# A chunked mLSTM feeding a two-layer MLP on one core: the program's head is reordered

## The chip, the cores and the metric

One core of one Trainium2 chip. The metric is the device time of one launch in microseconds (us). The kernel before took 427.0 us as the median of 3 runs (426.79 to 427.44).

## The reference

An mLSTM recurrence over 768 positions for 4 x 8 heads of width 40, and an MLP on its output:

```python
for t in range(S):
    m_new = max(f[t] + m, i[t])
    C = exp(f[t] + m - m_new) * C + exp(i[t] - m_new) * outer(v[t], k[t])
    n = exp(f[t] + m - m_new) * n + exp(i[t] - m_new) * k[t]
    y[t] = sigmoid(o[t]) * (C @ q[t]) / max(abs(n @ q[t]), 1)
x = y as 3072 rows of 320
h = x @ w_in                      # 320 x 2048
out = (h * sigmoid(h)) @ w_out    # 2048 x 320
```

Everything is float32 at the border of the kernel.

## The kernel before, in words

The recurrence is cut into 12 chunks of 64 positions, each in two halves of the batch: 24 **units** (class `Unit`, `u0`, `u1`, ...). A unit makes a matrix of exponents `e` (products with `sel`, `terms`, L433 to L446), exponentiates it to `D` (`expo_act`, L456), multiplies it with the scores `p` = q.k (`scores` L586, `weigh` L613), multiplies the result with v (`values` L641, output `po`), normalises (`norm`, `level`, L707 to L720), multiplies with the output gate (`scale`, L739, output `x`), and carries the state on (`state`, `hold`, `carry`). `xpose` (L856) transposes `x` into `px`; `xputs` (L865 to L872) copies `px` into the MLP's input. In the first MLP step the first 256 of the 320 features go as one float32 copy to `x0` (L865), the other 64 as a high part and a remainder to `xb` (L870, L872).

The MLP works in 8 **steps** (class `Step`) of three units, 384 rows each. In a step, `mm1(fc)` makes one of 16 **groups** of 128 hidden features: for step 0 two products over 256 rows of `w_in` (`wi`, the main part) and two over the remaining 64 rows (`wh`, the **tail**), all added up in one PSUM bank `ph` (L923). `act` takes tanh (L937, ScalarE) and the product with `ph` (`g`, L944, VectorE), and `mm2` multiplies `g` with `w_out` into `pout` (L1017), two groups behind `mm1`. `ph` has two banks, so group 2 needs the bank that `g` of group 0 gives back.

The weights arrive as 64-bit numbers in parts: `i0` to `i7` (w_in), `c0`, `c2`, `c4`, `c6` (tails, one for four groups), `o0` to `o7` (w_out), in the order of the string at L378. `load` issues a part's DMA on SyncE's queue (L283), `rise` widens its two halves on ScalarE (L291, L292), `make` puts them together on VectorE (L315), `halve` splits a tail part into a high part (phase 0, L336) and a remainder (phase 1, L338). `wload(n)` loads the next n parts, `wmake(n)` makes the next n and loads one more after each.

All engines run in the order in which the code is written (both `manual_schedule` lines at the top), each engine's queue in order. So the head, from `u0.load_qk()` to the table `FILL`, is a hand-written order: a call is placed where its instruction should stand in its engine's queue. `FILL[fc]` lists what is put behind group fc of step 0; `FILL[0]` makes the first w_out part, holds unit 2's state and exponentiates unit 3's reach; `FILL[1]` makes part `i2` and exponentiates unit 3 (`expo_act`); `FILL[2]` begins with the scores of unit 3, which take the one PSUM buffer of `couple` in which unit 3's exponents stood.

`gates` yields after each of its pieces, so that `run(1, two)` places one piece of the second pair of chunks (L175 to L193). `small(32)` and `warm(6, ph)` are products of constants with the identity, whose results nobody reads.

Of the kernel before, what the change touches and what calls it, by code (L numbers as in the profile page):

```python
# [8 lines left out]
F32 = mybir.dt.float32  # L9
# [36 lines left out]
def mlstm_mlp_kernel(  # L46
# [217 lines left out]
    class Part:  # L264
# [17 lines left out]
                to, src = self.raw, self.src  # L282
            nc.sync.dma_start(to, src)  # L283

        def rise(self):

            if not wide:
                return
            low, high = self.raw[:, :, :, 0], self.raw[:, :, :, 1]
            h32 = high.bitcast(F32)  # L290
            nc.scalar.activation(h32, h32, AF.Prelu, scale=2.0**-112, alpha=-(2.0**32))  # L291
            nc.scalar.activation(  # L292
                low, self.raw.bitcast(U8)[:, :, :, 3], AF.Copy, scale=1 / 32, bias=-31 / 64
            )
            self.risen = True

        def make(self):
            K, nb, n, nm = self.K, self.nb, self.n, self.nm
# [76 lines left out]
        )  # L375


    order = "c0 i0 i1 o0 i2 c2 o1 i3 o2 c4 i4 o3 i5 o4 c6 i6 o5 i7 o6 o7"  # L378
    parts = [part(x[0], int(x[1])) for x in order.split()]
    nload, nmade = [0], [0]  # L380

# [37 lines left out]
    class Unit:  # L419
# [438 lines left out]
        def xput(self, st):  # L858
            run(2, self.xputs(st))

        def xputs(self, st):
            n, px = self.n, self.px
            cs = slice(n % UPS * UT, (n % UPS + 1) * UT)
            if st.j == 0:
                nc.scalar.copy(st.x0[:, 0:2, cs], px[:, 0:2, :])  # L865
                a = slice(2, 3)
            else:
                a = slice(0, 3)
            hi, lo = st.xh[:, :, cs], st.xl[:, :, cs]
            nc.scalar.copy(hi, px[:, a, :])  # L870
            yield
            self.low = nc.vector.tensor_tensor(  # L872
                out=lo, in0=px[:, a, :], in1=hi.bitcast(F32), op=ALU.subtract
            )

    def run(n, it):
        for _ in range(n):
            next(it, None)

    def pieces(two, n):  # L880
        return (slice(0, n // 2), slice(n // 2, n)) if two else (slice(0, n),)

    class Step:


        def __init__(self, j):
            self.j = j

            if j == 0:
                self.x0 = pb.tile([128, 3, NT], F32, tag="big", name=f"x{j}")  # L890
                both = pb.tile([128, 2, NT], F32R, tag="big", name=f"xb{j}")
                self.xh, self.xl = both[:, 0:1, :], both[:, 1:2, :]
            else:
                self.xh = pb.tile([128, 3, NT], F32R, tag="big", name=f"xh{j}")
                self.xl = pb.tile([128, 3, NT], F32R, tag="big", name=f"xl{j}")
            self.g = {}
            self.po = None

        def mm1(self, fc):
            j = self.j  # L900
            fs = slice(fc * 128, (fc + 1) * 128)
            ph = psH.tile([128, NT], F32, tag="h", name=f"ph{j}_{fc}")
            if j == 0 and fc == 0:
                warm(6, ph)
            if j == 0:
                w = wi[fc // 2]
                b = fc % 2 * 128
                ops = [(w[:, a, b : b + 128], self.x0[:, a, :]) for a in range(2)]
            else:
                w = wl[fc // 2]  # L910
                b = fc % 2 * 128
                ops = []
                for a in range(2):
                    ops += [
                        (wh[:, a, fs], self.xh[:, a, :]),
                        (wh[:, a, fs], self.xl[:, a, :]),
                        (w[:, a, b : b + 128], self.xh[:, a, :]),
                    ]
            z = 2 * (j > 0)
            ops += [(wh[:, 2, fs], self.xh[:, z, :]), (wh[:, 2, fs], self.xl[:, z, :])]  # L920
            for i, (w, x) in enumerate(ops):
                for c in pieces(j == 0 and fc in (0, 1, 2, 3, 12, 13, 14) and i == 1, NT):
                    nc.tensor.matmul(  # L923
                        ph[:, c],
                        w,
                        x[:, c],
                        start=(i == 0),
                        stop=(i == len(ops) - 1),
                        skip_group_check=True,
                    )  # L930

            self.ph = ph
# [178 lines left out]
    u1.load_v()  # L1111
    u2.load_v()
    u1.load_ko()
    wload(2)
    u2.load_ko()
    wload(2)
    for _ in range(2):
        nc.tensor.matmul(
            dummy, ident, ident.unsqueeze(1).broadcast_to([128, 4, 128]), start=True, stop=True
# [7 lines left out]
    u1.mask()  # L1127
    u2.mask(psU.tile([128, H, L], F32, tag="u", name="e2"))
    u0.scores()
    small(32)  # L1130
    u0.expo()
    u0.expo_act()
    u0.keep()
# [26 lines left out]
    u1.place()  # L1160
    u1.values()
    u1.gate()
    u2.gate()
    u1.keys(nc.gpsimd)
    run(1, two)
    u1.norm()
    u1.level()
    u2.place()
    u2.values()
    u1.scale()  # L1170
    u2.keys(nc.gpsimd)
    u0.room()
    u0.xpose()
    u1.state()
    u3.mask(couple("e3")[:, :4, :].rearrange("p b (c t) -> p (b c) t", t=L))
    u3.expo()
    u2.norm()
    u2.level()
    wmake(1)
    u2.scale()  # L1180
    halve(0, nc.gpsimd)
    steps[0] = st = Step(0)
    u0.xput(st)
    u3.load_qk()
    wmake(1)
    u1.xpose()
    u3.reach()
    u1.xput(st)
    u2.room(psU, "u")
    u2.xpose()  # L1190
    u2.xput(st)
    u3.load_kvo()
    wmake(1)
    FILL = {
# [65 lines left out]
    for k in range(FIRST):  # L1260
        j, fc = divmod(k, NFC)
        st, at = steps[j], places(k)
        if j == 0 and fc in KEYS:
            units[KEYS[fc]].keys()
        st.mm1(fc)
        if 0 in at:
            def blocks():
                block(at[0].n)
# [286 lines left out]
```

## Time and profile before

| | |
|---|---|
| median of 3 runs | 427.0 us (426.79 to 427.44) |
| profiled execution | 426.86 us, of which the profile's span is 425.1 us |
| PE busy | 417.6 us, 98% (6864 matmuls, 6864 weight loads) |
| DVE, ACT, POOL busy | 65%, 52%, 31% |
| chain that ended last | PE 77%, "issue" 18%, DVE 2%, ACT 1%, DMA 1% |
| PEclk | 9 (90% or more) in all 40 slices |
| DMA | 57.60 MB; share 8 or 9 tenths in the first five slices |
| queue q8, instructions | 54 packets, 0.88 MB |

PE is TensorE's matrix unit, DVE VectorE, ACT ScalarE, POOL GpSimd, SP SyncE. A share of 98% says that there is little to win by hiding work, and that what PE does not do in time is paid at the end. Slice 1 of 40 is the one with less: PE shows 7 tenths there and 9 in nearly all others. That slice is the head.

### The profile page before, as it was taken

Reading aid. Unit: us, or ns where it says so; the run is one execution under the profiler, and the core shown is the slowest. Engines: PE = TensorE matmul, PEld = TensorE weight load, DVE = VectorE, ACT = ScalarE, POOL = GpSimd, SP = SyncE. Lnnn points to the kernel's source line nnn. Section 1 sums busy time; section 2 is a strip of 40 time slices with the busy share of each in tenths; the row PEclk is TensorE's granted clock in tenths of the full one; section 3 lists DMA queues with packets and bytes.
Section 4 is the critical chain, followed back from the end, with each engine's and each line's share of the span. In section 5 each row is a group of like instructions: output and inputs, shape, how many; then the busy total and the mean of one; then the engine's idle time right before and its main releaser. Section 6 shows DMA issues by size and latency. Waiting matters only on the chain.

```text
span 425.1 us, 16217 instructions
## 1 busy us (share of the span) xinstructions
PE 417.6 (98%) x6864; PEld 389.7 (92%) x6864; DVE 274.5 (65%) x575; ACT 223.0 (52%) x493; POOL 131.6 (31%) x140
## 2 busy tenths in 40 slices
PE   7999999999999999999999999999999999999995
PEld 4777779999999999999999999999999999999995
DVE  5879877987875667477655677466673676444442
ACT  7787777774654454445453544454454434443331
POOL 6754235424432444034431343134530210000000
PEclk9999999999999999999999999999999999999999
DMA  8999989365533755066630774246650321001001
GB/s 267 375 358 242 282 239 287 83 174 142 130 121 98 180 150 155 26 181 179 145 99 26 191 184 133 74 137 144 163 162 2 77 56 39 20 17 32 2 2 48
DMA packets 63401, 57.60 MB, mean 136 GB/s; under 512 B 31808, under 2 KB 49936, under 8 KB 63328
## 3 DMA queue, kind: packets, MB, share of 16 engines
q1 hardware_dynamic: 63056, 56.20, 47.8%
q8 instruction: 54, 0.88, 0.9%
q10 hardware_dynamic: 208, 0.26, 0.2%
q14 instruction: 19, 0.16, 0.1%
q0 software_dynamic: 64, 0.10, 0.1%
HBM read 49.09 MB, written 7.36 MB: 133 GB/s over the span
## 4 chain that ended last, share of the span: by engine, by line
PE 77%; issue 18%; DVE 2%; ACT 1%; DMA 1%; POOL 0%; POOLq 0%; DVEq 0%; ACTq 0%
PE spot L1322 28%; PE pout L1346 26%; PE ph L923 6%; PE pout L1017 6%; PE p L586 3%; PE p L679 2%; PE p L657 2%; PE spot L765 2%; DMA home<-in_ig_dram 1%; DVE D L613 0%; PE p L856 0%; PE px L856 0%; PE po L641 0%; POOL qt L570 0%; DVE home L188 0%
## 5 line engine op out<-in xcount | busy, mean ns | idle before, releaser
L1322 PE MATMUL spot<-xh,wh 64*128 64x384 f32 x660 | 148.7, 339 | 0.0
L1346 PE MATMUL pout<-woh,gh 64*128 64x320 f32 x648 | 128.0, 311 | 0.0
L1346 PE MATMUL pout<-woh,gl 64*128 64x320 f32 x648 | 126.5, 305 | 0.0
L1346 PE MATMUL pout<-wol,gh 64*128 64x320 f32 x648 | 126.1, 304 | 0.0
L961 ACT ACTIVATE th<-spot 128x384 f32<-128x384 f32 x110 | 54.1, 492 | 132.7 <-PE spot L1322 132.5
L1322 PE MATMUL spot<-xl,wh 64*128 64x384 f32 x550 | 122.8, 336 | 0.0
L981 DVE TENSOR_TENSOR gl<-th,gh 128x384 fp32r<-128x384 f32 x113 | 75.3, 666 | 54.9 <-ACT gh L977 44.3
L968 DVE SCALAR_TENSOR_TENSOR th<-th,spot 128x384 f32<-128x384 f32 x110 | 60.6, 551 | 64.1 <-ACT th L961 64.0
L1322 PEld LDWEIGHTS spot<-xh,wh 64*128 64x128 f32 x660 | 98.8, 184 | 2.2 <-ACTq L1302 0.3
L1322 PE MATMUL spot<-xh,wl 64*128 64x384 f32 x440 | 97.7, 333 | 0.0
L1346 PEld LDWEIGHTS pout<-woh,gh 64*128 64x128 f32 x648 | 88.8, 184 | 1.3
L1346 PEld LDWEIGHTS pout<-woh,gl 64*128 64x128 f32 x648 | 88.8, 184 | 0.0
L1346 PEld LDWEIGHTS pout<-wol,gh 64*128 64x128 f32 x648 | 88.6, 184 | 0.0
L977 ACT CAST gh<-th 128x384 fp32r<-128x384 f32 x113 | 58.0, 513 | 39.0 <-DVE th L968 32.8
L1322 PEld LDWEIGHTS spot<-xl,wh 64*128 64x128 f32 x550 | 76.5, 184 | 0.0
L1322 PEld LDWEIGHTS spot<-xh,wl 64*128 64x128 f32 x440 | 64.6, 184 | 0.0
L570 POOL TENSOR_TENSOR qt<-qk,lq 104x512 f32<-104x512 f32 x22 | 29.1, 1321 | 63.1 <-ACT lq L566 62.5
L810 POOL TENSOR_TENSOR Cm<-Cm,lq 104x328 f32<-104x328 f32 x19 | 18.4, 966 | 91.0 <-PE p L679 90.0
L545 POOL TENSOR_TENSOR am<-mask,aT 128x512 f32<-128x512 f32 x20 | 20.9, 1044 | 43.2 <-DVE kw L605 19.4
L553 POOL TENSOR_TENSOR D<-D,am 128x512 f32<-128x512 f32 x20 | 27.7, 1384 | 8.9 <-DMA D<-LFd 5.9
L1017 PE MATMUL pout<-wo,g 128*128 128x320 f32 (+1 forms) x120 | 27.0, 368 | 0.0
L923 PE MATMUL ph<-x,wi 128*128 128x384 f32 (+1 forms) x78 | 23.6, 432 | 0.0
(170 smaller groups left out, 544.9 us busy)
## 6 DMA issues: line engine op xcount, KB each, us to landing
qk<-in_qk_dram SPq DMA_DIRECT2D x24, 512.0 KB, 5.2
ko<-in_ko_dram SPq DMA_DIRECT2D x24, 320.0 KB, 5.1
wro<-in_w_out_dram SPq DMA_DIRECT2D x8, 640.0 KB, 6.3
wri<-in_w_in_dram SPq DMA_DIRECT2D x8, 512.0 KB, 7.4
D<-LFl SPq DMA_DIRECT2D x32, 128.0 KB, 3.5
lq<-LFl SPq DMA_DIRECT2D x32, 128.0 KB, 4.5
vb<-in_vp_dram SPq DMA_DIRECT2D x48, 82.0 KB, 4.7
out_dram<-ob SPq DMA_DIRECT2D x45, 80.0 KB, 2.2
```

Of the source, the lines that this page charges most:

```text
L545: return nc.gpsimd.tensor_tensor(out=self.am, in0=mask.unsqueeze(1).broadcast_to([128, H, L]), in1=aT[:, self.c, self.p, :].unsqueeze(2).b ...
L553: nc.gpsimd.tensor_tensor(out=self.Dm, in0=self.Dm, in1=self.am, op=ALU.add)
L570: nc.gpsimd.tensor_tensor(out=self.qt, in0=self.q[:KS], in1=self.lq[:KS], op=ALU.mult)
L810: nc.gpsimd.tensor_tensor(out=v, in0=heads(Cb[r, a]) if n == NP else v, in1=self.lq[r, :, L - 1].unsqueeze(2).broadcast_to([r.stop - r.sta ...
L923: nc.tensor.matmul(ph[:, c], w, x[:, c], start=(i == 0), stop=(i == len(ops) - 1), skip_group_check=True,)
L961: self.tanh = nc.scalar.activation(th, ph, AF.Tanh, scale=0.5)
L968: nc.vector.scalar_tensor_tensor(out=th, in0=th, scalar=1.0, in1=ph, op0=ALU.add, op1=ALU.mult)
L977: nc.scalar.copy(gh, th)
L981: nc.vector.tensor_tensor(out=gl, in0=th, in1=gh.bitcast(F32), op=ALU.subtract)
L1017: nc.tensor.matmul(self.po[t][:, c], g[:, ts], w[:, c], start=(fc == 0 and i == 0), stop=(last and i == len(ops) - 1), skip_group_check=(j ...
L1322: m = nc.tensor.matmul(spot[g][:, :NT], w, x, start=(h == 0 and i == 0), stop=(h == 1 and i == n - 1), skip_group_check=True,)
L1346: m = nc.tensor.matmul(st.po[t], g[half(h), t * UT : (t + 1) * UT], w[half(h)], start=(f == 0 and i == 0 and (p, h) in ((0, 0), (0, 1), (1 ...
```

## The change

The first two parts in the order of loads change places. The widening of `i0` is taken out of `wmake` and put ahead of unit 2's gate; that of `c0` is cut in two. Unit 2 is normalised before unit 1 is scaled. All three units are transposed before the first copy to the MLP's input, and the copies of the 256 features (`lift`) come ahead of the remainders. The tail's remainder goes from POOL to DVE. One piece of `gates` goes behind all that. `mm1` can make a group's main part and its tail apart: groups 0 and 1 are now main 0, main 1, tail 0, (state of unit 2), tail 1. `small(32)` and `warm(6, ph)` go.

```diff
-        def rise(self):
+        def rise(self, phases=(0, 1)):
...
-    order = "c0 i0 i1 o0 i2 c2 o1 i3 o2 c4 i4 o3 i5 o4 c6 i6 o5 i7 o6 o7"
+    order = "i0 c0 i1 o0 i2 c2 o1 i3 o2 c4 i4 o3 i5 o4 c6 i6 o5 i7 o6 o7"
...
+        def lift(self, st):
+            cs = slice(self.n % UPS * UT, (self.n % UPS + 1) * UT)
+            nc.scalar.copy(st.x0[:, 0:2, cs], self.px[:, 0:2, :])
+            self.lifted = True
...
-            if j == 0 and fc == 0:
-                warm(6, ph)
...
+            main = len(ops) - 2
             for i, (w, x) in enumerate(ops):
+                if (i >= main) not in ends:
+                    continue
...
     u1.load_ko()
-    wload(2)
+    wload(1)
     u2.load_ko()
-    wload(2)
+    wload(3)
...
     u0.scores()
-    small(32)
     u0.expo()
...
     u1.gate()
+    u1.keys(nc.gpsimd)
+    parts[0].rise()
     u2.gate()
-    u1.keys(nc.gpsimd)
-    run(1, two)
     u1.norm()
     u1.level()
     u2.place()
     u2.values()
-    u1.scale()
     u2.keys(nc.gpsimd)
+    u2.norm()
+    u2.level()
     u0.room()
     u0.xpose()
+    u1.scale()
     u1.state()
     u3.mask(couple("e3")[:, :4, :].rearrange("p b (c t) -> p (b c) t", t=L))
     u3.expo()
-    u2.norm()
-    u2.level()
-    wmake(1)
+    u1.xpose()
     u2.scale()
-    halve(0, nc.gpsimd)
-    steps[0] = st = Step(0)
-    u0.xput(st)
-    u3.load_qk()
-    wmake(1)
-    u1.xpose()
-    u3.reach()
-    u1.xput(st)
     u2.room(psU, "u")
     u2.xpose()
-    u2.xput(st)
+    u3.reach()
+    steps[0] = st = Step(0)
+    x0, x1, x2 = (u.xputs(st) for u in (u0, u1, u2))
+    run(1, x0)
+    parts[1].rise((0,))
+    run(1, x1)
+    wmake(1)
+    u3.load_qk()
+    run(1, x0)
+    u2.lift(st)
+    parts[1].rise((1,))
+    run(1, x2)
+    run(1, x1)
+    wmake(1)
+    run(1, x2)
+    halve(0, nc.gpsimd, (0,))
+    halve(0, nc.vector, (1,))
+    run(1, two)
     u3.load_kvo()
     wmake(1)
...
-        st.mm1(fc)
+        if k == 0:
+            st.mm1(0, (0,))
+            st.mm1(1, (0,))
+            st.mm1(0, (1,))
+        else:
+            st.mm1(fc, (1,) if k == 1 else (0, 1))
```

PE at the first two groups, before. In `ph0_1` the first figure is the step and the second the group; `x0` with `wi` is the main part, `xb` with `wh` the tail, `pu2` the state of unit 2 (its remaining rows repeat these two), and the first row stands for six with their weight loads:

```order
L1100 MATMUL ph0_0_526<-maskb_105,identb_104 128x384
L923 MATMUL ph0_0_526<-x0_472,wi0_481 128x384
L923 MATMUL ph0_0_526<-x0_472,wi0_481 128x192 x2
L923 MATMUL ph0_0_526<-xb0_473,wh_106 128x384 x2
L765 MATMUL pu2_u_542<-vb2_145,kw2_426 40x41 x2
L765 MATMUL pu2_o_543<-vb2_145,kw2_426 40x41 x2
L923 MATMUL ph0_1_581<-x0_472,wi0_481 128x384
L923 MATMUL ph0_1_581<-x0_472,wi0_481 128x192 x2
L923 MATMUL ph0_1_581<-xb0_473,wh_106 128x384 x2
L923 MATMUL ph0_2_607<-x0_472,wi1_522 128x384
```

And now:

```order
L935 MATMUL ph0_0_494<-x0_456,wi0_463 128x384
L935 MATMUL ph0_0_494<-x0_456,wi0_463 128x192 x2
L935 MATMUL ph0_1_498<-x0_456,wi0_463 128x384
L935 MATMUL ph0_1_498<-x0_456,wi0_463 128x192 x2
L935 MATMUL ph0_0_494<-xb0_457,wh_106 128x384 x2
L767 MATMUL pu2_u_508<-vb2_145,kw2_391 40x41 x2
L767 MATMUL pu2_o_509<-vb2_145,kw2_391 40x41 x2
L935 MATMUL ph0_1_498<-xb0_457,wh_106 128x384 x2
L935 MATMUL ph0_2_569<-x0_456,wi1_490 128x384
```

The six constant products are gone, and the main part of group 1 stands between the main part and the tail of group 0.

ACT from the gate of unit 1 (`ko1`) to the copies of unit 2, before (`wrc0` is the tail part, `wri0` the w_in part, `px` the transposed units):

```order
L559 ACTIVATE ko1_172<-ko1_172 128x320
L559 ACTIVATE ko2_178<-ko2_178 128x320
L291 ACTIVATE wrc0_174<-wrc0_174 128x256
L292 ACTIVATE wrc0_174<-wrc0_174 128x256
L865 COPY x0_472<-px0_428 128x2x128
L870 CAST xb0_473<-px0_428 128x128
L291 ACTIVATE wri0_176<-wri0_176 128x512
L292 ACTIVATE wri0_176<-wri0_176 128x512
L865 COPY x0_472<-px1_485 128x2x128
L870 CAST xb0_473<-px1_485 128x128
L865 COPY x0_472<-px2_509 128x2x128
L870 CAST xb0_473<-px2_509 128x128
```

And now:

```order
L561 ACTIVATE ko1_172<-ko1_172 128x320
L292 ACTIVATE wri0_174<-wri0_174 128x512
L294 ACTIVATE wri0_174<-wri0_174 128x512
L561 ACTIVATE ko2_176<-ko2_176 128x320
L866 COPY x0_456<-px0_398 128x2x128
L879 CAST xb0_457<-px0_398 128x128
L292 ACTIVATE wrc0_178<-wrc0_178 128x256
L866 COPY x0_456<-px1_427 128x2x128
L879 CAST xb0_457<-px1_427 128x128
L866 COPY x0_456<-px2_435 128x2x128
L294 ACTIVATE wrc0_178<-wrc0_178 128x256
L879 CAST xb0_457<-px2_435 128x128
```

The w_in part is widened ahead of unit 2's gate, and the tail part in two pieces between the copies.

DVE from the weighing of unit 2 (`D2`) on, before (of `norm`, `level` and `scale` only the first instruction is shown here; L188 is the piece of `gates`):

```order
L613 TENSOR_TENSOR D2_305<-p2_357,D2_305 128x512
L188 SCALAR_TENSOR_TENSOR home_110<-home_110 32x128
L707 TENSOR_SCALAR po1_386<-po1_386 128x8
L739 SCALAR_TENSOR_TENSOR x1_422<-ko1_172,po1_386 128x256
L707 TENSOR_SCALAR po2_405<-po2_405 128x8
L315 SCALAR_TENSOR_TENSOR wtc0_460<-wrc0_174 128x256
L739 SCALAR_TENSOR_TENSOR x2_464<-ko2_178,po2_405 128x256
L872 TENSOR_TENSOR xb0_473<-px0_428,xb0_473 128x128
L315 SCALAR_TENSOR_TENSOR wi0_481<-wri0_176 128x512
L872 TENSOR_TENSOR xb0_473<-px1_485,xb0_473 128x128
L872 TENSOR_TENSOR xb0_473<-px2_509,xb0_473 128x128
L315 SCALAR_TENSOR_TENSOR wi1_522<-wri1_180 128x512
```

And now:

```order
L615 TENSOR_TENSOR D2_273<-p2_325,D2_273 128x512
L709 TENSOR_SCALAR po1_354<-po1_354 128x8
L709 TENSOR_SCALAR po2_374<-po2_374 128x8
L741 SCALAR_TENSOR_TENSOR x1_402<-ko1_172,po1_354 128x256
L741 SCALAR_TENSOR_TENSOR x2_431<-ko2_176,po2_374 128x256
L317 SCALAR_TENSOR_TENSOR wi0_463<-wri0_174 128x512
L881 TENSOR_TENSOR xb0_457<-px0_398,xb0_457 128x128
L881 TENSOR_TENSOR xb0_457<-px1_427,xb0_457 128x128
L317 SCALAR_TENSOR_TENSOR wtc0_474<-wrc0_178 128x256
L340 TENSOR_TENSOR wh_106<-wtc0_474,wh_106 64x2x128 x2
L188 SCALAR_TENSOR_TENSOR home_110<-home_110 32x128
L317 SCALAR_TENSOR_TENSOR wi1_490<-wri1_180 128x512
```

Unit 2 is normalised right after unit 1, `wi0` comes ahead of all remainders, the tail's split (L340) is new here, and the gate piece went from the second place to the last but one.

## Rows read from the trace of the kernel before

**Rows 1.** Busy time by stretches: us, busy (x instructions) of each engine, PEclk, DMA.
```profile
5.00:10.00 5.00, 4.18 (x104) 2.93 (x102) 3.69 (x12) 3.31 (x7) 2.57 (x9) 1.00 1.05 339
...
30.00:35.00 5.00, 5.00 (x20) 3.53 (x19) 4.05 (x7) 4.89 (x13) 1.04 (x1) 1.00 0.98 229
```

**Rows 2.** PE in order of time, 24 to 28 us: start, us, what [idle before].
```profile
24.25 1.46 PE L923 MATMUL ph<-x,wi 128*128 128x384 f32 x6
...
25.89 1.78 PE L1017 MATMUL pout<-wo,g 128*128 128x320 f32 x6
27.77 0.69 PE L586 MATMUL p<-qk 40*64 40x64 f32 x32
```

**Rows 3.** ACT in order of time, 16 to 28 us.
```profile
16.23 0.47 ACT L559 ACTIVATE ko<-ko 128x320 f32<-128x320 f32 x1 [1.24 <-DMA ko<-in_ko_dram]
...
18.40 0.67 ACT L292 ACTIVATE wri<-wri 128x512 uint32<-128x512 uint8 x1
...
19.47 0.37 ACT L865 COPY x<-px 128x256 f32<-128x256 f32 x1
...
22.16 0.49 ACT L937 ACTIVATE th<-ph 128x384 f32<-128x384 f32 x1 [1.03 <-PE ph L923]
...
27.11 0.60 ACT L456 ACTIVATE D<-e 128x512 f32<-128x512 f32 x1
```

**Rows 4.** PE in order of time, 0 to 22 us.
```profile
1.36 3.71 PE L1118 MATMUL dummy<-ident 128*128 128x512 f32 x4 [1.36 <-POOL ident masks.py:199]
...
6.29 1.11 PE L1104 MATMUL dummy<-maskb,identb 128*128 128x64 bf16 x32
8.21 0.39 PE L442 MATMUL e<-terms,home 96*128 96x64 bf16 x8 [0.82 <-DVE terms L170]
...
13.39 0.73 PE L641 MATMUL po<-vb,D 128*64 128x82 f32 x16
14.68 0.79 PE L641 MATMUL po<-vb,D 128*64 128x82 f32 x16 [0.55 <-DVE po L707]
15.27 0.77 PE L641 MATMUL po<-Cb,qt 104*64 104x82 f32 x16
...
18.89 0.55 PE L856 MATMUL px<-ident,x 128*128 128x128 f32 x3
19.27 1.14 PE L1100 MATMUL ph<-maskb,identb 128*128 128x384 bf16 x6
20.25 1.53 PE L923 MATMUL ph<-x,wi 128*128 128x384 f32 x6
21.47 0.65 PE L923 MATMUL ph<-xb,wh 128*128 128x384 f32 x2
```

**Rows 5.** DVE in order of time, 13 to 23 us.
```profile
13.11 0.68 DVE L613 TENSOR_TENSOR D<-p,D 128x512 f32<-128x512 f32 x1
13.70 0.79 DVE L188 TENSOR_TENSOR_SCAN home<-home 32x128 f32<-32x128 f32 x1
...
16.23 0.17 DVE L707 TENSOR_SCALAR po<-po 128x8 uint32<-128x8 uint32 x1
...
16.87 0.50 DVE L720 TENSOR_TENSOR po<-po,den 128x320 f32<-128x320 f32 x1
...
17.73 0.68 DVE L739 SCALAR_TENSOR_TENSOR x<-ko,po 128x256 f32<-128x256 f32 x3
...
19.11 0.98 DVE L315 SCALAR_TENSOR_TENSOR wi<-wri 128x512 uint32<-128x512 uint32 x1 [0.49 <-ACT wri L292]
...
22.69 0.56 DVE L944 SCALAR_TENSOR_TENSOR g<-th,ph 128x384 f32<-128x384 f32 x1 [0.82 <-ACT th L937]
```

**Rows 6.** DMA queues from 11.9 to 14.6 us: packets, MB, share of 16 engines.
```profile
q8 instruction: 1, 0.02, 2.5%
```

**Rows 7.** POOL in order of time, 17 to 21 us.
```profile
17.89 0.85 POOL L336 CAST wh<-wtc 64x256 fp32r<-64x256 f32 x2 [0.82 <-DVE wtc L315]
18.82 1.87 POOL L338 TENSOR_TENSOR wh<-wtc,wh 64x256 fp32r<-64x256 f32 x2
```

More of the change, by code (lines that the diff above doesn't have):

```diff
@@ L290, in rise @@
             h32 = high.bitcast(F32)
[L291 to L295, printed above, removed]
+            if 0 in phases:
+                nc.scalar.activation(h32, h32, AF.Prelu, scale=2.0**-112, alpha=-(2.0**32))
+            if 1 in phases:
+                nc.scalar.activation(
+                    low, self.raw.bitcast(U8)[:, :, :, 3], AF.Copy, scale=1 / 32, bias=-31 / 64
+                )
+                self.risen = True
         def make(self):
@@ L864, in xputs @@
             if st.j == 0:
-                nc.scalar.copy(st.x0[:, 0:2, cs], px[:, 0:2, :])
+                if not hasattr(self, "lifted"):
+                    self.lift(st)
                 a = slice(2, 3)
@@ L895, in __init__, with mm1 @@
                 self.xl = pb.tile([128, 3, NT], F32R, tag="big", name=f"xl{j}")
-            self.g = {}
+            self.g, self.made = {}, {}
             self.po = None
-        def mm1(self, fc):
+        def mm1(self, fc, ends=(0, 1)):
             j = self.j
             fs = slice(fc * 128, (fc + 1) * 128)
-            ph = psH.tile([128, NT], F32, tag="h", name=f"ph{j}_{fc}")
-            if j == 0 and fc == 0:
-                warm(6, ph)
+            if 0 in ends:
+                self.made[fc] = psH.tile([128, NT], F32, tag="h", name=f"ph{j}_{fc}")
+            ph = self.made[fc]
             if j == 0:
```

## The prediction

> **What bounds the kernel now.** I read the stretches of five microseconds first, then PE in order of time, then ACT and DVE in order of time, and last the queues. From 30 us on PE is busy 5.00 of 5.00 us, while from 5 to 10 us it shows 4.18 [rows 1]. So the end moves one for one with the moment at which PE becomes continuous, and the head matters only through that moment. I call it the hinge; it is the start of unit 3's scores at 27.77 us. Two things come together there. PE's own queue is held by the product into `pout` until 25.89 + 1.78 = 27.67 us [rows 2]. And the scores take the PSUM buffer in which unit 3's exponents stand, so they also need ACT's exponential, 27.11 + 0.60 = 27.71 us [rows 3]. The two ends lie 0.04 us apart. After the change both must come earlier for a gain, and the later of them sets the loss.
>
> Going back along ACT: from the tanh of group 0 (`th`, 22.16) to the end of the exponential it works 5.55 us without a wait of note [rows 3], on the same instructions in the same order as after the change. So the hinge lies 5.6 us behind that tanh. The tanh waits 1.03 us for PE, that is for the first group, whose main part starts at 20.25 and whose tail starts at 21.47 [rows 3, 4]. That start waits for DVE: `wi0` is put together from 19.11 to 20.09 us [rows 5], behind the second widening on ACT, 18.40 + 0.67 = 19.07 [rows 3]; and that widening stood behind unit 2's gate, for whose load ACT stood idle 1.24 us until 16.23.
>
> **The change part by part.**
>
> *Constant products.* The 32 small ones take 1.11 us from 6.29 on, but the next products of weight, the exponents at 8.21, wait for DVE's `terms` [rows 4]. The six large ones (19.27, 1.14 us) fill the time in which PE waits for `wi0`. Taking them out gives 0 by itself; what hides it is DVE's work, and if DVE came earlier the six would cost up to 1.14. In the queue they are 38 matmuls and 38 weight loads fewer.
>
> *Loads.* SyncE issues the w_in part ahead of unit 2's gate load and the tail part behind it. ACT can widen the w_in part in its 1.24 us of idle time ahead of 16.23 (twice 0.67), and the gate moves to about 16.8 [rows 3]. Its user, the scaling of unit 2, comes after 18 us, as is shown below. Unit 2's gate load and the tail part may land later by one part; ACT's cover for the tail's widening is over 1 us, so I cost this at 0, and at up to 1 us if that cover is gone.
>
> *DVE ahead of the first product.* The scan of the gates (0.79 us [rows 5]) goes behind the whole chain. What is left between the end E of unit 2's values on PE and the start S of group 0's main part is 0.15 us of passing on, norm and level of unit 2 (16.23 to 17.37, 1.14 us), and the scalings of units 1 and 2, 0.68 each [rows 5]. That makes 2.65 us. Then two paths run side by side: the last of unit 2's transposes (0.3 of the 0.55 us [rows 4]) and its copy to `x0` on ACT (0.37 [rows 3]), or `wi0`, 0.98 us as it ran before [rows 5]. So S = E + 3.32 to E + 3.63, and with 0.1 of passing on E + 3.4 to E + 3.75; I take E + 3.5, since the 0.98 was measured while POOL did the tail's remainder, which is no longer there.
>
> *When unit 2's values end.* Before, the first half of these products starts at 14.68 after 0.55 us idle, and the second ends at 15.27 + 0.77 = 16.04 us [rows 4]. The releaser named, DVE's norm of unit 1, is no input: weighed `D2` is ready at 13.11 + 0.68 = 13.79 [rows 5], and unit 1's values end at 13.39 + 0.73 = 14.12. If nothing but inputs held these products, E would be 14.12 + 1.36 = 15.48. A packet of the instruction queue runs just then [rows 6], and I suspect that PE waits for its own program. In PE's queue 64 rows fewer would stand ahead, so the boundary would move to the last of the unit's 64 rows, and the wait would fall there rather than go. Bounds: 15.48 and 16.04, and 16.3 if the wait grows; I take 15.9, nearest to the row. The Trainium skill ("Runtime: NRT & Kernel Launch", Instruction fetch mechanics) says that the sequencer fetches the next block while it works on the current one and that a block's boundary costs almost nothing. By that the wait has another cause, E is 15.48, and the time by the sum below is 0.05 under the profiled 426.86, about 426.8; by the row it is 427.2.
>
> *The new order of the products.* Before, group 0's tail came 1.22 us behind its main part (20.25 to 21.47), and the tanh 0.69 behind the tail (21.47 to 22.16) [rows 3, 4]. Now group 1's main part, another 1.22, stands between. The tanh of group 0 starts at S + 1.22 + 1.22 + 0.69 = S + 3.13. With E = 15.48, S is 18.98 and the tanh at 22.11, 0.05 earlier than before; with 15.9 it is 22.53, 0.37 later; with 16.04 it is 22.67, 0.51 later. The corners are E = 15.48 with S = E + 3.4, a tanh at 22.01 (0.15 earlier), and E = 16.3 with E + 3.75, 23.18 (1.0 later).
>
> *The tail's split.* Its second phase goes from POOL (1.87 us for two [rows 7]) to DVE. Half of POOL's first phase is 0.43. From the copy of unit 2 (S) come the second half of the widening (some 0.45, two thirds of the 0.67 of 512 columns), putting together (some 0.4, by half of 0.98) and 0.43 of the cast, then 0.94 for a half of the remainder, were it as slow as on POOL: 2.2 us in all. The tail of group 0 is needed at S + 2.44. Covered, by 0.2; if the cover goes, the second half costs up to 0.94 + 0.43 = 1.37 us.
>
> **The sum.** PE then does group 1 earlier by 1.22 us and could reach unit 3's scores about 1 us ahead of ACT's exponential; but it has to wait for that, so the saved time turns into idle time of PE just ahead of the hinge. The hinge follows the tanh: 27.77 + 0.37 = 28.14. Against the profiled execution, 426.86 us (span 425.1 and 1.76 around it), this is 426.86 + 0.37 = 427.2 us. The median of the runs, 427.0, is 0.14 over that execution, within what I leave. A difference under 0.2%, 0.85 us, can't be told from none here; the forecast is no change, with its own range 426.7 (0.15 earlier) to 427.9 (1.0 later).
>
> **Rivals.**
>
> *The hinge is PE's.* If the exponential is not what releases the scores, or ACT gets to it sooner, then the group of `ph` at 24.25 [rows 2] sets the stream. It needs the bank that `g` of group 0 gives back, at 22.69 + 0.56 = 23.25, 1.09 us behind the tanh [rows 5]. With the tanh at 22.11 to 22.53 group 2 starts at 23.2 to 23.6, 0.6 to 1.05 earlier than 24.25, and the time is 425.8 to 426.3; with E = 15.48 it is 425.8. For it: PE waited for nothing else in this stretch, and its end is only 0.04 us ahead of ACT's. Against it: ACT has no idle time between tanh and exponential to take out. Its condition, then, is ACT going faster than its 5.55 us.
>
> *Slower: the new order puts the tail and group 1 on ACT's path.* Its place is the tanh of group 0, and its price is the 1.22 us of group 1's main part now ahead of it, with nothing won before it. If S is later than 19.88, by E = 16.3 together with `wi0` at its old 0.98, or a tail that is not ready, the tanh starts after 23.0 and the loss passes 0.85; at the corner, 23.18, the time is 427.9, and with a late tail 428.3. For it: `wi0` did take 0.98, and the wait on PE may grow. Against it: both have to go wrong at once.
>
> *Slower: the clock.* Without the small products PE stands idle some 1.9 us from 6.35 to 8.21. The clock granted is 1.00, the full 2.4 GHz, in both stretches [rows 1]. If it fell to the half level, 1.2 GHz, for a stretch as long as the first constant products (3.71 us [rows 4]), half of that stretch's work, 1.85 us, would be left over, and the time 428.7. For it: those first products, which come after idle time, take 1.81 ns a column (3.71 us for 4 x 512), against 0.79 for a main part (1.22 us for two of 384 and four of 192 columns), though they are not the same kind of product. Against it: PE has stood idle for 1.36 us before the first of them and for 0.82 us ahead of 8.21 without a stretch below 1.00 that I read. The Trainium skill ("TensorE: Matmul & The Clock Gate", Part 1) says that the clock is held at half until the engine has been active and goes back when it idles, which would make the constant products useful; no row here shows a fall.
>
> *It does not do what it says.* If the w_in part lands no earlier, ACT's widening only swaps places with the gate's wait; S still goes by DVE, and the time is in the forecast's range.
>
> **How the numbers follow.** The forecast, no change at 427.2, gets 0.63, which holds the last rival. The hinge that is PE's gets 0.15 at 425.8; the late tail and group 1 get 0.14 at 428.0; the clock 0.08 at 428.7. So faster 0.15, same 0.63, slower 0.22. The range, 425.7 to 428.3, takes in the first three cases and leaves out the clock and the tails.
>
> **What would show it.** In the profile of the changed kernel: group 0's main part starts at 19 to 19.5 instead of 20.25; its tanh lies between 22.0 and 22.7, about 3.1 behind; the scores of unit 3 start right behind the end of ACT's exponential, with PE idle some 1 us before them; the wait in unit 2's values has moved to their end or is gone; `wi0` is begun at about 18; the granted clock is 1.00 in every stretch from 5 us on. The tail `wh` is ready before group 0's tail is reached. The forecast is wrong if the scores start before 27.0 or after 28.7, and the reason is wrong, whatever the time, if ACT is idle between the tanh and the exponential.

## The result and the profile after

The changed kernel took 430.83 us, the median of 7 runs (429.32 to 433.86), beside 427.0 us before: a ratio of 1.0098 with a 95% interval of 1.0069 to 1.0128. It is slower by about 1%, outside the range given (425.7 to 428.3), and the forecast of no change was wrong. The profiled execution took 430.34 us, with a span of 428.6 us, 3.5 us longer than before.

PE in order of time shows where the loss begins; the rows answer to [rows 2, 4]:

```profile
8.18 0.39 PE L444 MATMUL e<-terms,home 96*128 96x64 bf16 x8 [1.13 <-DVE terms L170]
...
10.85 1.13 PE L588 MATMUL p<-qk 40*64 40x64 f32 x32
11.91 1.36 PE L643 MATMUL po<-vb,D 128*64 128x82 f32 x16
...
15.37 1.91 PE L643 MATMUL po<-vb,D 128*64 128x82 f32 x32
17.12 0.73 PE L643 MATMUL po<-Cb,qt 104*64 104x82 f32 x16
...
21.30 2.86 PE L935 MATMUL ph<-x,wi 128*128 128x384 f32 x12 [0.21 <-DVE xb L881]
23.86 0.64 PE L935 MATMUL ph<-xb,wh 128*128 128x384 f32 x2
...
30.13 0.69 PE L588 MATMUL p<-qk 40*64 40x64 f32 x32 [0.63 <-ACT D L458]
```

The exponents start as before (8.18 against 8.21). But the sixteen products of unit 0's values take 1.36 us (11.91), and before they took 0.79:

```profile
11.22 0.79 PE L641 MATMUL po<-vb,D 128*64 128x82 f32 x16
```

Unit 2's values end at 17.12 + 0.73 = 17.85 us, 1.81 later than the 16.04 of before. The busy time by stretches says why; the column PEclk is the granted clock:

```profile
8.00:9.50 1.50, 1.32 (x20) 0.81 (x20) 0.78 (x3) 0.56 (x2) 0.00 (x0) 1.00 1.01 300
9.50:13.00 3.50, 3.50 (x68) 2.84 (x66) 1.82 (x4) 2.57 (x8) 2.63 (x3) 0.54 1.01 302
13.00:16.50 3.50, 3.50 (x70) 3.20 (x70) 1.73 (x5) 0.84 (x2) 2.25 (x5) 0.50 1.04 384
16.50:18.00 1.50, 1.50 (x38) 1.41 (x35) 1.14 (x5) 1.48 (x4) 0.76 (x2) 0.96 1.05 394
30.00:35.00 5.00, 4.87 (x49) 3.75 (x50) 3.91 (x8) 4.81 (x15) 2.77 (x3) 1.00 0.98 252
```

From about 9.8 to 16.6 us the clock is at half, 1.2 GHz. A PE that shows 3.50 of 3.50 us busy there is slow, not well used: the busy column alone hides it. From 17 us on the clock is full again, so only seven microseconds are hit. Six of the seven runs had a mean clock of 0.986 to 0.992; the seventh, at 1.00, took 429.32 us, still 2.3 us over the kernel before. ACT behind it reads as forecast, 1.68 us of wait and then the tanh, and the exponential at the end:

```profile
24.55 0.49 ACT L949 ACTIVATE th<-ph 128x384 f32<-128x384 f32 x1 [1.68 <-PE ph L935]
...
29.47 0.60 ACT L458 ACTIVATE D<-e 128x512 f32<-128x512 f32 x1
```

The hinge, unit 3's scores, is at 30.13 instead of 27.77, 2.36 us late. The span grew by 3.5, so another 1.1 us is lost behind it, in a part that the change does not touch. ACT's tanh of the 21st, 41st and 61st group shows where; first before, then after:

```profile
94.21 0.49 ACT L961 ACTIVATE th<-spot 128x384 f32<-128x384 f32 x1 [0.20 <-PE spot L1322]
...
156.75 0.49 ACT L961 ACTIVATE th<-spot 128x384 f32<-128x384 f32 x1 [0.51 <-PE spot L1322]
...
218.59 0.49 ACT L961 ACTIVATE th<-spot 128x384 f32<-128x384 f32 x1 [0.52 <-PE spot L1322]
```

```profile
96.55 0.49 ACT L973 ACTIVATE th<-spot 128x384 f32<-128x384 f32 x1 [0.20 <-PE spot L1347]
...
159.41 0.49 ACT L973 ACTIVATE th<-spot 128x384 f32<-128x384 f32 x1 [0.51 <-PE spot L1347]
...
222.09 0.49 ACT L973 ACTIVATE th<-spot 128x384 f32<-128x384 f32 x1 [0.52 <-PE spot L1347]
```

The distance is 2.34, then 2.66, then 3.50 us. It is flat from the hinge to 148 us of the time before, grows in three steps (0.32 us at 149, 0.46 in two parts at 185 and 198, 0.37 at 211), and is flat to the end.

### The profile page after: what moved, and what is told of

Its sections match the earlier page's. It is cut to its first block, busy times and chain, and to the rows that moved or that the text cites. A ratio compares the mean times of both kernels' runs of the same rounds, so it can differ in the third digit from the quotient of the medians.

```text
span 428.6 us, 16140 instructions
## 1 busy us (share of the span) xinstructions
PE 420.3 (98%) x6826; PEld 390.8 (91%) x6826; DVE 275.4 (64%) x577; ACT 222.7 (52%) x493; POOL 130.6 (30%) x138
## 4 chain that ended last, share of the span: by engine, by line
PE 78%; issue 17%; ACT 1%; DVE 1%; DMA 1%; POOL 0%; POOLq 0%; DVEq 0%; ACTq 0%
PE spot L1347 28%; PE pout L1371 25%; PE ph L935 6%; PE pout L1029 6%; PE p L588 4%; PE p L681 2%; PE p L659 2%; PE spot L767 1%; PE po L643 1%; DMA home<-in_ig_dram 1%; PE pu L779 0%; PE e L448 0%; PE p L858 0%; PE e L444 0%; POOL qt L572 0%
## 5 line engine op out<-in xcount | busy, mean ns | idle before, releaser
L1347 PEld LDWEIGHTS spot<-xh,wh 64*128 64x128 f32 x660 | 99.8, 184 | 2.4 <-ACTq L1327 0.3
L555 POOL TENSOR_TENSOR D<-D,am 128x512 f32<-128x512 f32 x20 | 28.6, 1430 | 3.5 <-DVE g L956 1.9
```

Of the source, the lines that this page charges most:

```text
L555: nc.gpsimd.tensor_tensor(out=self.Dm, in0=self.Dm, in1=self.am, op=ALU.add)
L1347: m = nc.tensor.matmul(spot[g][:, :NT], w, x, start=(h == 0 and i == 0), stop=(h == 1 and i == n - 1), skip_group_check=True,)
```

## The experiments

Three theories had to be told apart: the **clock** (it falls because the constant products are gone), the **blocks of PE's program** (76 rows of its queue fewer, products and weight loads, so blocks end at other products, and PE stands where one arrives late), and the **new order** itself.

Each row below is read from the profiled execution: E is the end of unit 2's values, "hinge" the start of unit 3's scores. The last two columns are of the timed runs; each ratio is to runs of the kernel before taken beside them, whose median was 426.89 to 427.20 us.

| kernel | E | hinge | hinge - E | median us | ratio to before (95%) |
|---|---|---|---|---|---|
| before | 16.04 | 27.77 | 11.73 | 427.0 | |
| changed | 17.85 | 30.13 | 12.28 | 430.83 | 1.0098 (1.0069 to 1.0128) |
| a1_small | 15.26 | 27.54 | 12.28 | 428.33 | 1.0030 (1.0011 to 1.0050) |
| a2_wide | 16.79 | 29.10 | 12.31 | 429.15 | 1.0039 (1.0022 to 1.0057) |
| b1_nosmall | 16.44 | 28.14 | 11.70 | 428.98 | 1.0037 (1.0016 to 1.0059) |
| a3_small_exp | 15.60 | 27.19 | 11.59 | 427.52 | 0.9996 (0.9975 to 1.0017) |
| b3_nowarm | 15.64 | 27.86 | 12.22 | 427.61 | 1.0023 (1.0004 to 1.0043) |
| a4_small_tail | 16.35 | 27.84 | 11.49 | 427.21 | 0.9999 (0.9984 to 1.0014) |
| a5_rows | 15.26 | 26.85 | 11.59 | 426.85 | 0.9997 (0.9973 to 1.0021) |
| a7_early | 14.91 | 27.37 | 12.46 | 428.04 | 1.0032 (1.0011 to 1.0053) |
| a8_rows_ahead | 15.86 | 27.45 | 11.59 | 427.23 | 1.0010 (0.9994 to 1.0027) |
| before_again | 16.00 | 27.69 | 11.69 | 426.69 (one run) | |
| after_again | 17.36 | 29.65 | 12.29 | 429.35 (one run) | |
| a1_again | 15.38 | 27.94 | 12.55 | 427.16 (one run) | |

**The small products back** (a1_small).

```diff
     u0.scores()
+    small(32)
     u0.expo()
```

> The changed kernel with the 32 small constant products back at their old place; the six large ones stay out. Clock theory: the granted clock, 0.50 from about 9.7 to 16.8 us in the changed kernel, is 1.00 again from 5 us on; group 0 starts at about 19.4 instead of 21.30, its tanh at about 22.5 instead of 24.55, unit 3's scores at about 28.1 instead of 30.13, and the time is 427.0 to 427.8. Rival, the new order itself costs the time: the clock is repaired but the tanh stays after 24.0 and the time stays over 429. Third theory, on what the changed kernel loses behind the hinge (three steps of 0.32, 0.46 and 0.37 us at 149, 198 and 211 us): if they come from PE's queue being 76 rows shorter, so that the blocks of the program end elsewhere, they change place or go now that it is only 12 rows shorter; if they come from late data, they stay.

The clock is 1.00 throughout. In this execution the second 16 products of unit 2's first half run on without a wait:

```profile
13.23 1.30 PE L643 MATMUL po<-vb,D 128*64 128x82 f32 x32
14.47 0.79 PE L643 MATMUL po<-Cb,qt 104*64 104x82 f32 x16
...
18.71 2.86 PE L935 MATMUL ph<-x,wi 128*128 128x384 f32 x12 [0.21 <-DVE xb L881]
...
27.54 0.69 PE L588 MATMUL p<-qk 40*64 40x64 f32 x32 [0.64 <-ACT D L458]
```

The hinge is at 27.54, even ahead of before and 0.56 us earlier than expected, because E is early (15.26) in this execution. So the rival that the new order costs all of it falls. The three steps are gone; one of 0.50 us came at 132 us. The time is not quite that of before, though: the median is 1.1 us over that of the runs beside it, and over the 427.0 to 427.8 expected.

**Wide products in their place** (a2_wide), and **the kernel before without its small products** (b1_nosmall).

```diff
     u0.scores()
+    warm(4)
     u0.expo()
```

> The changed kernel with four constant products of 512 columns at the place of the 32 small ones: about as many columns, but 8 rows of PE's queue instead of 64. Clock theory: the clock stays at 1.00 as with the small ones, and unit 3's scores start within 0.3 us of those with the small ones. Program-block theory: the three steps behind the hinge stay as in the changed kernel (about 1.1 us together), because the queue is still 68 rows shorter, so the time is about 428 to 428.6. Late-data theory: no steps, 427.0 to 427.6.

```diff
     u0.scores()
-    small(32)
     u0.expo()
```

> The kernel before with only its 32 small constant products taken out. Clock theory: the granted clock falls to 0.50 somewhere between 8 and 12 us and comes back some 7 us later; the time is 1.5 to 4 us longer, 428.5 to 431. Rival, the products are mere filler and the order costs the time: 426.8 to 427.4, no change. Program-block theory alone (64 rows fewer, clock unchanged): 427 to 428.2 with steps far behind the head.

Both held a surprise. In a2_wide the clock is full and PE is busy through 7 and 8 us, and yet the hinge is 1.56 us behind a1_small's, where 0.3 was expected. PE in order of time, of a2_wide and then of b1_nosmall:

```profile
13.43 1.30 PE L643 MATMUL po<-vb,D 128*64 128x82 f32 x32
14.67 0.61 PE L643 MATMUL po<-Cb,qt 104*64 104x82 f32 x11
16.36 0.43 PE L643 MATMUL po<-Cb,qt 104*64 104x82 f32 x5 [1.08 <-issue]
```

```profile
14.47 0.75 PE L641 MATMUL po<-Cb,qt 104*64 104x82 f32 x15
16.16 0.28 PE L641 MATMUL po<-Cb,qt 104*64 104x82 f32 x1 [0.94 <-issue]
```

In the middle of a run of like products PE stops for about a microsecond, for nothing that the profile can name ("issue"). The place counts rows: a2_wide has 8 rows more ahead than b1_nosmall, four products with their weight loads, and its wait comes four products sooner (11 done instead of 15). The kernel before has 64 rows more than b1_nosmall, 32 products, and its wait [rows 4] stands 31 or 32 products sooner, ahead of the second sixteen. In b1_nosmall the work of the other engines is that of before, and yet PE passes the old place without a wait (13.23, 32 products in one row of 1.30 us). So a wait for unit 1's normalisation, which the profile names, is ruled out, and the likely cause is that a block of PE's program ends there. The trace doesn't say whose program a packet of q8 brings. Its 54 packets, 0.88 MB, come to 64 bytes for each of PE's 13728 rows, and with 76 rows fewer there are 53, which fits PE's. The length of the wait follows the one instruction packet of this stretch [rows 6], whose starts the trace gives:

| | packet starts | PE goes on | wait |
|---|---|---|---|
| a3_small_exp | 11.44 | 14.24 | 0.27 |
| before | 12.18 | 14.68 | 0.55 |
| a4_small_tail | 12.52 | 14.99 | 1.03 |
| b1_nosmall | 13.83 | 16.16 | 0.94 |
| a2_wide | 13.93 | 16.36 | 1.08 |

PE goes on 2.3 to 2.8 us behind the packet's start, whatever the products. In a1_small (10.90) and a5_rows (11.13) the packet was early enough for no wait at all. With 56 to 64 rows fewer ahead, it starts 1.3 to 3 us later. In the changed kernel's profile the packet starts at 13.19 and no wait shows: at half clock PE is among these last products only from 17.12 on, too late to need to wait.

The same count of rows fixes a place far behind the head. The expectation that a2_wide keeps the three steps missed: it has two, 0.27 us at 185 and 0.69 at 198, and b1_nosmall, in the old order, has two at the same times, 0.33 and 0.56. PE near the second, of b1_nosmall and then of a2_wide:

```profile
195.21 0.35 PE L679 MATMUL p<-Cm,qt 40*64 40x41 f32 x10
195.87 0.31 PE L679 MATMUL p<-Cm,qt 40*64 40x41 f32 x4 [0.31 <-issue]
```

```profile
196.10 0.41 PE L681 MATMUL p<-Cm,qt 40*64 40x41 f32 x12
196.90 0.31 PE L681 MATMUL p<-Cm,qt 40*64 40x41 f32 x2 [0.39 <-issue]
```

By here a2_wide has 4 rows fewer ahead than b1_nosmall (68 against 64 fewer than before), two products, and it stops two products later. So the order of the head doesn't place these stops; the row count does.

b1_nosmall's profile kept the full clock, so the expectation of a fallen one missed there; the 0.37 us that the hinge lost are the longer wait, and 0.92 us more come from the steps behind it. But in 6 of its 12 timed runs the mean clock was 0.987 to 0.992 (the changed kernel's profile, with its seven microseconds at half, has 0.989). Those six took 429.07 to 431.81 us (median 429.40), the other six 427.59 to 428.89 (median 428.10).

**The exponential off the path** (a3_small_exp).

```diff
     u3.load_kvo()
     wmake(1)
+    u3.expo_act()
+    u3.keep()
...
-        1: lambda: (run(2, near), wmake(1), u3.expo_act(), u3.keep(), u3.near(), u4.load_qk()),
+        1: lambda: (run(2, near), wmake(1), u3.near(), u4.load_qk()),
```

> The changed kernel with the 32 small products back and unit 3's exponential (with the copy behind it) moved on ACT ahead of group 0's tanh, where ACT stands idle. Theory of the prediction, that unit 3's scores wait for this exponential at the end of ACT's 5.6 us: PE no longer waits there, the scores start when PE gets to them, 0.5 to 1.1 us earlier than with the small products alone, and the time is 426.2 to 427.0. Rival, that PE or the output product sets the hinge: no gain, within 0.2 us.

PE no longer waits at the hinge (the row has no idle time in front of it):

```profile
14.24 0.79 PE L643 MATMUL po<-vb,D 128*64 128x82 f32 x16 [0.27 <-DVE po L709]
14.84 0.77 PE L643 MATMUL po<-Cb,qt 104*64 104x82 f32 x16
...
27.19 0.69 PE L588 MATMUL p<-qk 40*64 40x64 f32 x32
```

Counted from E, which moves with the packet, it gained 12.28 - 11.59 = 0.69 us, within the 0.5 to 1.1 forecast. The hinge was ACT's in the changed order.

**The large products alone** (b3_nowarm).

```diff
-            if j == 0 and fc == 0:
-                warm(6, ph)
```

> The kernel before with only its six large constant products taken out: 12 rows fewer in PE's queue, behind unit 2's values. Program-block theory (a block of PE's program that arrives late costs time where short products run fast): nothing changes at unit 2's values (0.55 us of wait as before) and the hinge stays within 0.1 us, but the later blocks end elsewhere, and the step of about 0.5 us at 136 us that the changed kernel with the small products shows appears here too; the time is 427.2 to 427.9. Rival, the step comes from the new order or from data: no step, 426.8 to 427.3. Clock theory: the clock stays at 1.00, because the 32 small products are still there.

The step at 132 us appears, in the kernel before, by the loss of six products that nobody reads. PE there, of b3_nowarm and then of a1_small, which lacks the same twelve rows:

```profile
132.63 0.35 PE L679 MATMUL p<-Cm,qt 40*64 40x41 f32 x10
133.24 0.31 PE L679 MATMUL p<-Cm,qt 40*64 40x41 f32 x4 [0.25 <-issue]
```

```profile
132.35 0.35 PE L681 MATMUL p<-Cm,qt 40*64 40x41 f32 x10
132.94 0.31 PE L681 MATMUL p<-Cm,qt 40*64 40x41 f32 x4 [0.24 <-issue]
```

Both stop ahead of the last four of 32 products, in two kernels of different order. Before, these products run through in one row of fourteen. But so they do in a4_small_tail (below), which also lacks twelve rows and shows no step here; first before, then a4_small_tail:

```profile
132.57 0.41 PE L679 MATMUL p<-Cm,qt 40*64 40x41 f32 x14
```

```profile
132.67 0.41 PE L681 MATMUL p<-Cm,qt 40*64 40x41 f32 x14
```

So the row count sets the place at which PE may have to stop, and the order does not; whether and how long it stops changes from execution to execution. The packets fit: in a1_small one starts at 130.49 us and PE goes on 2.45 us behind it, at 132.94; in a4_small_tail it starts at 130.57, and PE, 0.3 us later at these products, comes to the place at about the time at which it could go on. The wait in unit 2's values was not 0.55 us as expected but gone (E = 15.64), as the packet started at 11.42.

**Group 0's tail ahead again** (a4_small_tail), with the small products.

```diff
             st.mm1(0, (0,))
+            st.mm1(0, (1,))
             st.mm1(1, (0,))
-            st.mm1(0, (1,))
+            st.ph = st.made[0]
```

> The changed kernel with the 32 small products back and group 0's tail again ahead of group 1's main part. Theory of the prediction: group 0's tanh starts 1.0 to 1.25 us earlier than with the small products alone (21.95), at 20.7 to 21.0, unless the tail's weights are not ready (they would then add up to 0.7); ACT's exponential then ends earlier than PE reaches unit 3's scores, and the scores start 0.4 to 0.7 us earlier than 27.54; the time is 426.4 to 427.2 in the profiled execution. Rival, that the new order of the products is worth its place: the scores start no earlier than 27.4.

The absolute times missed: the block's wait took 1.03 us here, and the tail waited 0.23 us for its weights, which DVE had not split yet.

```profile
14.99 0.79 PE L643 MATMUL po<-vb,D 128*64 128x82 f32 x16 [1.03 <-DVE den L714]
...
21.59 0.59 PE L935 MATMUL ph<-xb,wh 128*128 128x384 f32 x2 [0.23 <-DVE wh L340]
```

From E the hinge is 11.49 us away against 12.28: the order of the products, undone, gives back 0.79 us. That is about as much as moving the exponential (0.69), and in both kernels PE no longer waits for ACT at the hinge.

**Rows restored behind the block's end** (a5_rows), and **ahead of it** (a8_rows_ahead). a5_rows is a3_small_exp with six short constant products ahead of group 0; a8_rows_ahead has them with the 32.

```diff
+            if j == 0 and fc == 0 and 0 in ends:
+                for _ in range(6):
+                    nc.tensor.matmul(ph[:, :L], identb, maskb, start=True, stop=True)
```

> As the kernel with the small products and the earlier exponential, and with six short constant products in the 0.21 us of idle time ahead of group 0: PE's queue is again as long as before from there on. Program-block theory: the step of 0.38 us at 136 us goes, no step is left but that of the kernel before, and the profiled execution gains 0.5 to 0.65 us on the kernel before, 426.2 to 426.5. Rival: the step stays, and the time is as without the six products (426.67 profiled).

> As the kernel with the small products, the earlier exponential and six short products ahead of group 0, but the six stand with the 32, so that all of PE's queue is as long as before from the first unit on. Program-block theory: the block ends 6 products earlier in unit 2's values than with 32, the later blocks end as in the kernel before, so no step appears at 132 us and none but that of the kernel before behind; in the head a wait of 0 to 1 us at the block's end. The profiled execution is 425.9 to 426.9, the median at or below that of the kernel before by 0 to 0.6 us. Rival, the gain of the earlier exponential was the luck of one execution: no better than the kernel before, 427.0 to 427.6, with unit 3's scores not before 27.6.

In a5_rows the step at 132 us is gone, and of the gain of 0.92 us at the hinge 0.84 are left at the end: 426.02 us in the profiled execution, where before had 426.86 (426.2 to 426.5 expected). In the timed runs it is not to be told from before (0.9997, 0.9973 to 1.0021). a8_rows_ahead also lacks the step at 132, but its profile has one of 0.5 us at 317 us, which no other kernel showed at that size, and its median is 0.3 us over that of the runs of before beside it, where 0 to 0.6 less was expected. Neither version beats the kernel before by what these runs can tell.

**The small products at another place** (a7_early): nearly as many rows (4 fewer than a1_small), but the idle time around 7 us open again.

```diff
-    for _ in range(2):
+    for _ in range(1):
         nc.tensor.matmul(
...
+    small(32)
     u0.scores()
     u0.expo()
```

> The changed kernel with the 32 small products placed ahead of unit 0's scores, and one of the two long constant products at the start left out in exchange: PE's queue is about as long as with the small products at their old place, so the blocks end as there, but the idle time of PE around 7 to 8 us stays open. Clock theory: the granted clock falls below 1.00 between 8 and 17 us, in the profile or in most of the timed runs (mean clock 0.985 to 0.993), and the time is 429 to 431. Program-block theory alone: the clock does not matter, and the time is as with the small products at their old place, 427.2 to 428.6, with a hinge within 0.4 us of 27.5.

The profile shows a full clock and a hinge at 27.37. But 5 of the 12 timed runs had a mean clock of 0.987 to 0.992, and those five took 429.46 to 430.92 us (median 429.99), the seven others 426.72 to 428.49 (median 427.13). Within one kernel, and so with the same rows, the runs of low clock are 2.9 us longer; in b1_nosmall the same comparison gives 1.3. "Most of the runs" was too much. In the 69 runs of a1_small, a2_wide, a3_small_exp, a4_small_tail, a5_rows and a8_rows_ahead, which all have constant products between the scores and the exponents, one mean clock was under 0.993.

**Three kernels profiled again**, unchanged.

> The kernel before, unchanged, one more look. Program-block theory: the place of the wait in unit 2's values is fixed by the number of PE's instructions ahead (ahead of the second 16 products of the first half), but its length follows the start of the instruction packet: PE goes on 2.3 to 2.8 us after that start, and does not wait at all if the packet starts by about 11.1 us. So the wait may be anywhere from 0 to 1 us here, at that place alone. Rival, the wait is for data (unit 1's normalisation, as the trace names it): it is 0.55 us again whatever the packet does.

> The changed kernel, unchanged, one more look. Clock theory: mean clock 0.986 to 0.992 again, with 0.50 for 6 to 8 us from about 10 us on, and unit 3's scores 2 to 3.5 us later than before. If the clock is not fallen in this execution, the program-block theory says that PE waits about 1 us at the last rows of unit 2's values, as in the kernel with four wide products, and the scores start 1.0 to 1.5 us later than before. In both cases steps of 0.7 to 1.2 us together between 130 and 215 us. Rival, the reordering itself: the same loss in the head whatever the clock and the packet.

> The changed kernel with the 32 small products back, one more look, since its profiled execution (427.39) was among the fastest of its runs (median 428.33). Program-block theory: the slower runs have a wait at the block's end in unit 2's values, of up to 1 us, wherever the instruction packet starts later than 11.1 us, and the same step at 132 us; 427.4 to 428.6. Rival: the head is as in the first look and the difference lies elsewhere.

The changed kernel had the fallen clock again (mean 0.989, 0.50 from 9 to 15.8 us), its hinge at 29.65, 21.90 us behind the first exponents as in the first execution (21.95), and two steps together of 0.6 us instead of three (0.7 to 1.2 expected). The kernel before took 426.69 us with its packet at 11.96 and the wait at the same place. It was 0.55 us long again, as the rival had it, so this run alone doesn't tell the two apart. a1_again took 427.16 us, so the slower runs of that kernel weren't caught; its packet started at 11.63, which is later than the 11.1 that was expected to be the limit, and E was 15.38 without a wait of note. Its step at 132 us is 0.27 us instead of 0.50. What makes a1_small's median 0.9 to 1.2 us longer than its two profiled executions stays open; the mean clock was 0.997 to 1.000 in all its runs but the slowest (0.994).

## Why the prediction was wrong

*The chain behind E was right.* Group 0 starts 3.45 us after unit 2's values (21.30 - 17.85; forecast 3.5), its tanh 3.25 later (3.13), and the scores 5.58 after the tanh (5.6). ACT has no idle time in between, as forecast, and PE stands 0.63 us before the scores (some 1 us forecast). The prediction said that with E unchanged at 16.04 the new order would cost 0.51 us; the runs have 12.28 - 11.73 = 0.55 (0.73 in a7_early and 0.82 in a1_again, by the 12.46 and 12.55 of the table). Where E is early this price shrinks: in b3_nowarm, the old order with E = 15.64, group 0 stands 1.30 us for `wi0` and the distance is 12.22, so there the new order loses nearly nothing. The tail's split was covered, as forecast: no wait stands ahead of 23.86.

*The step that failed is the term "Constant products", taken at 0.* It asked only what the products hide, and not that they keep the clock up and place the ends of PE's blocks. In the profiled execution the clock is 1.81 us of the loss, and the blocks are the likeliest cause of 1.12 more. The fall of the clock stood among the rivals with 0.08 and 1.85 us. It should have been the likely case: the changed kernel's mean clock is 0.986 to 0.992 in 6 of 7 runs. That E lost 1.81 us, nearly the 1.85, is luck: the price assumed 3.71 us at half clock and idle time of 1.9 us ahead of it, and the profile has 6.8 us at half clock behind 1.13 us of idle time; part of the slower work fell into the 0.8 us for which PE had waited there before. The argument against the fall was that PE had stood idle for 0.82 us ahead of the exponents and 1.36 us at the start without one. But ahead of the 0.82 us the products had filled the time until 7.40 [rows 4]. And the 1.36 us prove nothing: the clock's records in that trace begin at 4.88 us, although the view shows 1.00 before it, and the products ahead of it are the slow ones (1.81 ns a column). What decides is not settled. The gap ahead of the exponents is 1.13 us in the changed kernel, 0.96 in a7_early and 0.55 in b1_nosmall's profile, and the last two fell in about half of their runs. From 5 to 10 us PE is busy for 3.87 us in the changed kernel, 4.18 before [rows 1], and 3.80 in a7_early's profile, which kept the full clock. The Trainium skill ("TensorE: Matmul & The Clock Gate", Part 1) says that an idle engine goes back to the half clock; the 0.50 in the trace agrees in the level.

*The term "When unit 2's values end" had the right cause and was mis-sized.* With 56 or 64 rows fewer ahead the wait did move to the last products (a2_wide, b1_nosmall). It was allowed to reach 16.3; in a2_wide, at full clock, E is 16.79, 0.75 us later than before (one execution of each). In the changed kernel's profile the half clock alone makes the 1.81 us, since no wait shows; the two overlap, and the fall adds 1.06 us to what the later block costs at full clock. The Trainium skill ("Runtime: NRT & Kernel Launch", Instruction fetch mechanics) calls the cost of a block's end mostly hidden; here it was none in some executions and 0.27 to 1.08 us in others, and the measurement decides.

*What no term held are the blocks behind the hinge.* "So the end moves one for one with the hinge" is wrong by 1.1 us: 76 rows fewer shift every later block's end, and some then fall into or near runs of very short products. That PE works these off faster than its program comes is likely and not shown. b3_nowarm, a2_wide and b1_nosmall show that the row count places the stops at 132 us and at 198. For the three steps of the changed kernel it is the likeliest cause: they are gone in a1_small, with 64 of the rows back.

The sum is then 1.81 (clock, with the first block's 0.75 hidden in it) + 0.55 (order) + 1.12 (behind the hinge, taken as the rest) = 3.48 us, the growth of the profiled execution. The timed runs give the clock about half of the loss. Against the runs of before beside them, the medians are 1.1 us longer in a1_small (new order, 12 rows fewer), 1.9 in a2_wide (68 rows fewer, full clock) and 3.8 in the changed kernel, whose one run at full clock is 2.3 longer. The intervals of the first two overlap, so that the rows make a difference in the timed runs is not shown. The rival that the hinge is PE's fell: moving ACT's exponential gained 0.69 us. The slower rival of a late tail named the right place, the order ahead of the tanh, but its price was the 0.55 of the forecast.

## What to carry to other kernels

A product whose result nobody reads can do two things that its own time doesn't show: it keeps the clock up, and it sets where the blocks of the program end. Before such filler is taken out, the stretch behind it is to be read with the granted clock, and the profile after is to be compared at landmarks all the way to the end, since a shift in row count shows up far from the edit. When a kernel with filler wide but few is put against one with filler short and many, the two effects come apart: a2_wide kept the clock (0.995 to 1.000 in nine runs) and lost the place of the blocks.

## What was not expected of the hardware

- A wait that the profile puts down to another engine, "DVE po" or "DVE den", was in all likelihood for PE's own program: same row count, same product, with none to 1.03 us from execution to execution. Where it isn't at the start of a group of products the profile says "issue" instead.
- The instruction packet of one and the same place started anywhere from 10.90 to 12.52 us in kernels with equally many rows ahead. What sets that start is open. The load of the data queue q1 was full all along (102.8 to 103.3% of the 16 engines' time from 11 to 17 us in three kernels), so it couldn't be compared with an empty one.
- The clock falls in some executions of a kernel and not in others (a7_early 5 of 12, b1_nosmall 6 of 12, the changed kernel 6 of 7). It was seen low in one of 83 timed runs of the kernel before (0.992, 429.76 us), so its small products make the fall rare and don't exclude it.
